# Gated recurrence and squared-ReLU network on one core: weights fetched ahead, a shorter decode, and VectorE's order written by hand

## The chip, the cores and the metric

The kernel runs on one core of one Trainium2 chip. The time is device microseconds of one execution; the median of several is compared. The engines are TensorE (PE; its weight loads are PEld in the profile), VectorE (DVE), ScalarE (ACT), GpSimd (POOL) and SyncE (SP), which here only issues transfers. Each engine takes its instructions in its own order and waits on semaphores for the others.

## The reference

Two parts follow one another. The first is a gated recurrence over 4 sequences of 768 steps with 8 heads of width 48; the second a feed-forward network on the 3072 tokens.

```python
mag = np.sqrt(a_re * a_re + a_im * a_im)
scale = np.minimum(mag, 0.999) / (mag + 1e-06)
a_re_n, a_im_n = (a_re * scale, a_im * scale)
for t in range(S):
    new_re = ar * S_re - ai * S_im          # ar, ai: the gates of step t, per head and row
    new_im = ar * S_im + ai * S_re
    S_re, S_im = (new_re + k[t] (x) v[t], new_im)
    y[:, :, t] = q[t] @ S_re
...
x = y as (3072 tokens, 384)
h = np.maximum(x @ w_in, 0.0)               # w_in: 384 x 2048
out = (h * h) @ w_out                       # w_out: 2048 x 384
```

`w_in` and `w_out` come as 64-bit floats; all else is 32-bit.

## The kernel before

`quotient_path` does the work; `general_path` is a second version, entered at the end only when some gate lies outside the range in which quotients of running products are exact enough (`good` counts the partitions where all is in range).

**Groups.** A chunk is 128 steps of one sequence, with its 8 heads side by side. A group is two chunks, of two sequences; there are 12 groups. `make_operands(gi)` (L515) prepares a group on VectorE with a little help of ScalarE: the inverse magnitude of the gates, two scans of the clamped scale (`u`, `v`), running complex products of the gates in blocks of 8 steps (the steps with tile `pr`), then over blocks (four `cmul` levels), then across (`carry` and one large `cmul`), and last the operands `qk`. What of `qk` belongs to rows that share a partition with other heads goes through SP transfers to the tiles `last` and `prod`. `chunk(gi, b)` (L592) then has TensorE make the scores `a_ps` (L613), VectorE mask them to `a`, TensorE add them into `y` (L621) beside the contribution of the running state (L606), and ScalarE copy `y` to `x` (L626). For the next chunk TensorE transposes the keys (`tp`, L634), sums them with the values (`add`, L645), and VectorE updates `state`. `fill_gaps(i)` (L669) moves rows of `x` into the gaps by six SP transfers; after it `first_product(i)` (L676: TensorE into `h_ps`, ScalarE Relu and Square) and `second_product(i)` (L689: TensorE into `o_ps`, ScalarE copy, SP store) can run.

**Weights.** After group 0's attention `load_w1` and `load_w2` fetch the weights as words and `decode` (L449) turns each 64-bit float into a 32-bit one with seven VectorE instructions: 12 tiles of 512 columns for `w_in`, 16 of 384 for `w_out`, through two buffers of words.

**Order.** The program is written in one order, and a planner places the instructions of every engine by that order as a priority and by expected times; each engine then runs its list in order. PSUM has two banks each for `a_ps`, `h_ps` and the tiles `tp` and `add`, one each for `y` and `o_ps`. `raw`, which holds a group's inputs, has two buffers, so that `load(gi + 2)` may go when group gi's operands are done.

Of the kernel before, what the change touches and what calls it, by code (L numbers as in the profile page):

```python
# [33 lines left out]
A_RE, A_IM, Q, K, V = range(5)  # L34

# [310 lines left out]
def quotient_path(ctx, tc, feat, vtok, w_in, w_out, w1, w2, out, n_seq, good):  # L346
# [14 lines left out]
    NB = C // L  # L361
    assert C == P and DM == HH * NP * D == NG * P and PAD * NG == D and n_seq % GC == 0
# [5 lines left out]
    ops = ctx.enter_context(tc.tile_pool(name="ops", bufs=2))  # L368
# [8 lines left out]
    def rows(hh):  # L377
        return slice(hh * ROWS, hh * ROWS + D)

    def pads(hh):  # L380
        return slice(hh * ROWS + D, (hh + 1) * ROWS)
# [3 lines left out]
              for bp in range(n_seq // GC) for c in range(NCH)]  # L385

# [6 lines left out]
    def load(gi):  # L393
        for part in (slice(A_RE, Q), slice(Q, V)):
            for b, n in enumerate(groups[gi]):
                for hh in range(HH):
                    nc.sync.dma_start(out=raw[gi % 2][rows(hh), part, b],
                                      in_=feat[n, hh, :, part, 0:NG])
                    rest = feat[n, hh].rearrange("(g r) x p t -> g r x p t", g=NG)
                    for g in range(NG):  # L400
                        nc.sync.dma_start(out=raw[gi % 2][pads(hh), part, b, g],  # L401
                                          in_=rest[g, :, part, NG])
# [4 lines left out]
    load(0)  # L407
# [17 lines left out]
    last = [const.tile([P, 4, GC, C], F32, name=f"last{i}") for i in range(2)]  # L425
    prod = [const.tile([P, 2, GC, NP], F32, name=f"prod{i}") for i in range(2)]

# [8 lines left out]
    ends = const.tile([P, 2, NGR, SEG], F32, name="ends")  # L436


    def w1_views(w):
        cut = NG * HH * D  # L440
        main = w[0:cut].rearrange("(g hh d) f -> hh d g f", g=NG, hh=HH)
        rest = w[cut:DM].rearrange("(hh g r) f -> hh r g f", hh=HH, g=NG)
        return [(rows(hh), main[hh]) for hh in range(HH)] + [
            (pads(hh), rest[hh]) for hh in range(HH)]

    def w2_view(w):
        return w.rearrange("(fb p) m -> p fb m", p=P)

    def decode(dst, words, width):  # L449


        low, high = words[:, 0:width, 0], words[:, 0:width, 1]
        mant = nrm.tile([P, E], I32, tag="low", name="mant")[:, 0:width]
        nc.vector.tensor_scalar(out=mant, in0=high, scalar1=0xFFFFF, scalar2=0x100000,
                                op0=ALU.bitwise_and, op1=ALU.bitwise_or)
        value = mant.bitcast(F32)
        nc.vector.scalar_tensor_tensor(out=value, in0=low.bitcast(U32), scalar=2.0 ** -32,  # L457
                                       in1=mant, op0=ALU.mult, op1=ALU.add)
        power = nrm.tile([P, E], I32, tag="high", name="power")[:, 0:width]
        nc.vector.tensor_scalar(out=power, in0=high, scalar1=20, scalar2=0x7FF,  # L460
                                op0=ALU.logical_shift_right, op1=ALU.bitwise_and)
        nc.vector.tensor_scalar(out=power, in0=power, scalar1=896, scalar2=896 + 255,
                                op0=ALU.max, op1=ALU.min)
# [33 lines left out]
    def tt(out, in0, in1, op):  # L497
        nc.vector.tensor_tensor(out=out, in0=in0, in1=in1, op=op)  # L498
# [286 lines left out]
```

## Time and profile before

| | |
|---|---|
| median of 3 runs | 856.02 us (853.28 to 858.97) |
| the profiled execution | 858.16 us, span 856.2 us |
| busy in the span: PE, DVE, ACT, POOL | 720.8, 528.4, 248.2, 33.3 us |
| mean granted TensorE clock | 0.919 |
| from HBM, to HBM | 36.18 MB, 4.72 MB |

The span is what the profile shows between its first and last event; about 2 us lie around it. In a row of a timeline stand start and length in us, engine, line of the kernel, operation, output and inputs, and the count of merged instructions; the bracket behind it tells how long the engine was idle before and what released it. In a group's row stand busy time and the mean of one instruction in ns, then the idle time ahead of such instructions. Most VectorE instructions have line 498, that of the helper `tt`, and are told apart by their tiles.

### The profile page before, as it was taken

How to read it: one execution, taken by the hardware profiler on the slowest of the kernel's cores; microseconds unless marked ns; L12 is line 12 of the kernel's file. 1: busy time of each engine (PE TensorE's matmuls, PEld its weight loads, DVE VectorE, ACT ScalarE, POOL GpSimd, SP SyncE). 2: the span in 40 equal slices, each digit the busy share in tenths (PEclk: the TensorE clock that was granted, in tenths of full speed). 3: DMA queues.
4: the chain of work that ended last, by engine and by line, in shares of the span. 5: the costliest groups of instructions: out<-in, count | busy, mean ns of one | idle time of the engine just before them, and what ended most of it. 6: DMA issues, size and time to landing. Idle time of an engine off the chain costs nothing.

```text
span 856.2 us, 11195 instructions
## 1 busy us (share of the span) xinstructions
PE 720.8 (84%) x4154; PEld 536.5 (63%) x4154; DVE 528.4 (62%) x1131; ACT 248.2 (29%) x446; POOL 33.3 (4%) x44
## 2 busy tenths in 40 slices
PE   0035575579399999889999999999999999999997
PEld 0034353136378687577686776867868778678683
DVE  4993899989989989778977494793854002010000
ACT  3021121013225144325052351532613314114140
POOL 3100000020000100000100010010000000000000
PEclk9975677569689999989999999999999999999999
DMA  4323554413131132213222231221101100000000
GB/s 109 76 65 75 125 146 129 129 49 82 44 88 33 30 97 57 64 36 84 60 73 67 62 74 39 40 73 33 33 9 37 17 19 5 10 10 5 19 0 24
DMA packets 76095, 47.66 MB, mean 56 GB/s; under 512 B 40576, under 2 KB 72448, under 8 KB 76032
## 3 DMA queue, kind: packets, MB, share of 16 engines
q1 hardware_dynamic: 76032, 46.86, 21.8%
q8 instruction: 35, 0.57, 0.3%
q14 instruction: 28, 0.23, 0.1%
HBM read 36.18 MB, written 4.72 MB: 48 GB/s over the span
## 4 chain that ended last, share of the span: by engine, by line
PE 56%; DVE 28%; SPq 7%; DMA 4%; ACT 3%; issue 2%; DVEq 0%; ACTq 0%
PE o_ps L693 21%; PE h_ps L682 20%; PE a_ps L613 5%; DVE raw L498 5%; PE y L621 4%; DVE pr L498 4%; PE y L606 3%; SPq L401 2%; DVE sq L541 2%; DMA words<-in_moe_w_in_dram 2%; PE add L645 2%; DVE power L466 2%; DVE qk L498 2%; DVE mant L457 1%; DVE w L468 1%
## 5 line engine op out<-in xcount | busy, mean ns | idle before, releaser
L682 PE MATMUL h_ps<-x,w 128*128 128x256 f32 x1152 | 273.8, 396 | 27.5 <-DVE w L468 26.1
L693 PE MATMUL o_ps<-w,h 128*128 128x384 f32 x768 | 269.7, 506 | 21.3 <-DVE w L468 20.3
L682 PEld LDWEIGHTS h_ps<-x,w 128*128 128x128 f32 x1152 | 223.7, 197 | 68.7 <-issue 16.9
L693 PEld LDWEIGHTS o_ps<-w,h 128*128 128x128 f32 x768 | 147.1, 196 | 131.1 <-DVE w L468 28.1
L498 DVE TENSOR_TENSOR a<-a_ps,mask 128x512 f32<-128x512 f32 x48 | 31.4, 685 | 143.0 <-PE a_ps L613 142.8
L685 ACT ACTIVATE h<-h_ps 128x512 f32<-128x512 f32 x96 | 57.0, 594 | 146.5 <-PE h_ps L682 146.4
L613 PE MATMUL a_ps<-qk 48*128 48x128 f32 x576 | 54.3, 300 | 44.3 <-DVE qk L498 44.3
L498 DVE TENSOR_TENSOR pr<-raw 128x384 f32<-128x384 f32 x84 | 72.0, 857 | 21.1 <-DMA raw<-in_feat_dram 19.3
L613 PEld LDWEIGHTS a_ps<-qk 48*128 48x128 f32 x576 | 46.0, 203 | 51.8 <-DVE qk L498 44.3
L686 ACT ACTIVATE h<-h 128x512 f32<-128x512 f32 x96 | 60.4, 630 | 2.8
L696 ACT COPY o<-o_ps 128x384 f32<-128x384 f32 x24 | 11.5, 479 | 160.8 <-PE o_ps L693 160.6
L621 PE MATMUL y<-a,vt 128*64 128x128 f32 x384 | 40.4, 304 | 18.6 <-DVE a L498 18.4
L544 POOL COPY ends<-sq 128x6 f32<-128x6 f32 x24 | 25.8, 1074 | 587.8 <-DVE sq L541 553.5
L621 PEld LDWEIGHTS y<-a,vt 128*64 128x64 f32 x384 | 28.1, 150 | 29.1 <-DVE a L498 24.0
L606 PE MATMUL y<-qk,state_mm 128*128 128x128 f32 x240 | 34.9, 293 | 13.3 <-DVE qk L498 13.2
L498 DVE TENSOR_TENSOR raw<-pr 128x96 f32<-128x96 f32 x168 | 44.8, 331 | 1.7
L751 DVE CAST count<-number 1x1 int32<-1x1 f32 x1 | 0.1, 147 | 72.5 <-PE number L750 72.5
L498 DVE TENSOR_TENSOR qk<-raw 128x1536 f32<-128x1536 f32 x24 | 41.2, 1753 | 5.3 <-PE a_ps L613 5.2
L606 PEld LDWEIGHTS y<-qk,state_mm 128*128 128x128 f32 x240 | 32.5, 204 | 18.9 <-issue 13.4
L626 ACT COPY x<-y 128x512 f32<-128x512 f32 x24 | 14.1, 587 | 60.1 <-PE y L621 60.0
L645 PE MATMUL add<-vt,kt 128*64 128x48 f32 x640 | 28.4, 230 | 1.6 <-ACT kt L636 1.6
L645 PEld LDWEIGHTS add<-vt,kt 128*64 128x64 f32 x640 | 26.3, 144 | 5.0 <-ACT kt L636 2.4
(300 smaller groups left out, 598.7 us busy)
## 6 DMA issues: line engine op xcount, KB each, us to landing
raw<-in_feat_dram SPq DMA_DIRECT2D x96, 144.0 KB, 2.6
words<-in_moe_w_out_dram SPq DMA_DIRECT2D x16, 384.0 KB, 3.0
raw<-in_feat_dram SPq DMA_DIRECT2D x288, 16.0 KB, 2.0
vt<-in_vtok_dram SPq DMA_DIRECT2D x24, 192.0 KB, 3.2
last<-qk SPq DMA_DIRECT2D x72, 64.0 KB, 2.4
words<-in_moe_w_in_dram SPq DMA_DIRECT2D x24, 192.0 KB, 3.4
out_dram<-o SPq DMA_DIRECT2D x24, 192.0 KB, 1.9
words<-in_moe_w_in_dram SPq DMA_DIRECT2D x24, 64.0 KB, 3.3
```

Of the source, the lines that this page charges most:

```text
L401: nc.sync.dma_start(out=raw[gi % 2][pads(hh), part, b, g], in_=rest[g, :, part, NG])
L466: nc.vector.scalar_tensor_tensor(out=power, in0=high, scalar=-2 ** 31, in1=power, op0=ALU.bitwise_and, op1=ALU.bitwise_or)
L498: nc.vector.tensor_tensor(out=out, in0=in0, in1=in1, op=op)
L544: nc.gpsimd.tensor_copy(out=ends[:, i, gi], in_=x.rearrange("p (s t) -> p s t", t=C)[:, :, C - 1])
L606: nc.tensor.matmul(y[:, p_], lhsT=s[:, c, p_].rearrange("p hh e -> p (hh e)"), rhs=operand(c, p_, slice(0, P)), start=(p_ == 0 and c == RE ...
L613: nc.tensor.matmul(ps[hh][:, p_], lhsT=operand(2 + c, p_, rows(hh)), rhs=operand(c, p_, rows(hh)), start=(c == RE), stop=(c == IM))
L621: nc.tensor.matmul(y[hh * ROWS:(hh + 1) * ROWS, p_], lhsT=v[:, HH * p_ + hh], rhs=am[hh][:, p_], start=(first and p_ == 0), stop=(p_ == NP ...
L645: nc.tensor.matmul(add[rr, c, p_], lhsT=kt[c][:, p_, rr], rhs=v[:, HH * p_ + hh, 0:D], start=True, stop=True)
L682: nc.tensor.matmul(ps[:, j], lhsT=w1[:, g, (2 * f + j) * P:(2 * f + j + 1) * P], rhs=x_of[i][:, g], start=(g == 0), stop=(g == NG - 1))
L685: nc.scalar.activation(out=h, in_=ps, func=AF.Relu)
L686: nc.scalar.activation(out=h, in_=h, func=AF.Square)
L693: nc.tensor.matmul(ps, lhsT=h_of[i][f // 2][:, f % 2, b * C:(b + 1) * C], rhs=w2[:, f], start=(f == 0), stop=(f == NFB - 1))
```

## The change

- **Loads.** `load` moves all four inputs of a chunk in one transfer per half (and one per gap piece), where there were two. For group 0 the gates come first, their gap pieces issued by ScalarE.
- **Words.** Weights come in 16 blocks of 768 columns (256 columns of `w_in` in its three row groups, or two row groups of `w_out`) through three buffers; the first three are fetched at the start, and each decoded block fetches the one three further on.
- **Decode.** Five VectorE instructions instead of seven. It is right only for weights of moderate size, so ScalarE watches the range: a Square and an Abs_reciprocal_sqrt per block, each with a sum, go into `sizes`, which enters `good`. `general_path` now decodes the weights again by the old seven instructions (`decode_weights`), inside the branch.
- **Operands.** The seven steps in blocks stand between the parts of the magnitude chain instead of behind it. The gate product at a chunk's end is a 129th column of `qk` and travels with `last`, so the transfers of `prod` go; ScalarE copies it to `prod`. The copies of `ends` move from GpSimd to ScalarE.
- **Order.** `chunk` pauses at two points. For groups 0 and 1 VectorE's order is as written: blocks of `w_in` are decoded among the pieces of group 0's attention, blocks of `w_out` among those of group 1's, where each decoded block at once goes into second product 0, for both chunks, in two accumulators (`po`'s bank and one of the two of `ph`). From group 2 on the planner orders VectorE as before.

```diff
-    def load(gi):
-        for part in (slice(A_RE, Q), slice(Q, V)):
-            for b, n in enumerate(groups[gi]):
...
+    def load(gi):
+        load_parts(gi, slice(A_RE, V), nc.sync)
+        load_values(gi)
+
+    load_parts(0, slice(A_RE, Q), nc.scalar)
+    load_parts(0, slice(Q, V), nc.sync)
+    load_values(0)
     load(1)
...
+        nc.vector.tensor_scalar(out=head, in0=high, scalar1=3, scalar2=0x3FFFFFF8,
+                                op0=ALU.logical_shift_left, op1=ALU.bitwise_and)
+        nc.vector.scalar_tensor_tensor(out=head, in0=high, scalar=-2 ** 30, in1=head,
                                        op0=ALU.bitwise_and, op1=ALU.bitwise_or)
+        nc.vector.tensor_scalar(out=rest, in0=head, scalar1=-2 ** 23, scalar2=None,
+                                op0=ALU.bitwise_and)
+        rest = rest.bitcast(F32)
+        nc.vector.scalar_tensor_tensor(out=rest, in0=low.bitcast(U32), scalar=2.0 ** -52, in1=rest,
+                                       op0=ALU.mult, op1=ALU.mult)
+        tt(dst, head.bitcast(F32), rest, ALU.add)
+        size = nrm.tile([P, E], F32, tag="z", name="size")
+        nc.scalar.activation(out=size, in_=high.bitcast(F32), func=AF.Square,
+                             accum_out=sizes[:, 0, j:j + 1])
+        nc.scalar.activation(out=size, in_=size, func=AF.Abs_reciprocal_sqrt, bias=tiny,
+                             accum_out=sizes[:, 1, j:j + 1])
...
+        words = words_of[j] = dec.tile([P, E, 2], I32, name="words", bufs=3)
...
+    def weights(j):
+        if j in words_of:
+            k = j - NBLK
+            decode(w1[:, :, j * BLK:(j + 1) * BLK] if k < 0 else
+                   w2[:, 2 * k:2 * k + 2].rearrange("p k m -> p (k m)"), words_of[j], j)
+        if j + 3 < 2 * NBLK:
+            fetch(j + 3)
+
+    for j in range(3):
+        fetch(j)
...
         for hh in range(HH):
             for g in range(NG):
                 at = slice(hh * ROWS + g * PAD, hh * ROWS + (g + 1) * PAD)
-                nc.sync.dma_start(out=last[gi % 2][at], in_=qk[pads(hh), :, :, g])
-                nc.sync.dma_start(out=pd[at, :, :, NG:NP], in_=pd[pads(hh), :, :, g:g + 1])
+                nc.sync.dma_start(out=last[gi % 2][at, :, :, 0:C + 1],
+                                  in_=qk[pads(hh), :, :, g, 0:C + 1])
+        nc.scalar.copy(out=pd[:, :, :, 0:NG], in_=qk[:, 0:2, :, :, C])
+        nc.scalar.copy(out=pd[:, :, :, NG], in_=last[gi % 2][:, 0:2, :, C])
...
+    def attention_among(gi, others):
+
+        make_operands(gi)
+        first, second = [chunk(gi, b) for b in range(GC)]
+        for step, n in ((first, 3), (first, 0), (second, 2), (second, 0), (first, 1), (second, 0)):
+            next(step, None)
+            for _ in range(n):
+                next(others)
+        load(gi + 2)
+        fill_gaps(gi)
...
+    def second_weights():
+        for b, pool, tag in ((0, po, "o"), (1, ph, "h")):
+            banks[b] = pool.tile([P, DM], F32, tag=tag, name="o_ps")
+        for j in every:
+            weights(NBLK + j)
+            for b in range(GC):
+                second_product(0, b, banks[b], [j])
+            yield
+
+    with tc.manual_schedule(engines={mybir.EngineType.DVE}):
+        others = first_weights()
+        attention_among(0, others)
+        first_product(0, every[:6])
+        for j in every[6:]:
+            next(others)
+            first_product(0, [j])
+        others = second_weights()
+        attention_among(1, others)
+        for j in every[6:]:
+            next(others)
+            first_product(1, every[4 * (j - 6):4 * (j - 6) + 4])
+        for b in range(GC):
+            store(0, b, banks[b])
+    for gi in range(2, NGR + 1):
+        if gi < NGR:
+            attention(gi)
+        if gi > 2:
+            first_product(gi - 1, every)
+        for b in range(GC):
             ps = po.tile([P, DM], F32, tag="o", name="o_ps")
...
+            second_product(gi - 1, b, ps, every)
+            store(gi - 1, b, ps)
```

More of the change, by code (lines that the diff above doesn't have):

```diff
@@ L436, in quotient_path @@
     ends = const.tile([P, 2, NGR, SEG], F32, name="ends")
[L439 to L463, printed above, removed]
-        nc.vector.tensor_scalar(out=power, in0=power, scalar1=896, scalar2=2 ** 23,
-                                op0=ALU.subtract, op1=ALU.mult)
-        nc.vector.scalar_tensor_tensor(out=power, in0=high, scalar=-2 ** 31, in1=power,
-                                       op0=ALU.bitwise_and, op1=ALU.bitwise_or)
-        nc.vector.scalar_tensor_tensor(out=dst, in0=value, scalar=2.0 ** -20,
-                                       in1=power.bitcast(F32), op0=ALU.mult, op1=ALU.mult)
@@ L699, in quotient_path @@
[L699 to L714 removed]
+            h_of[i, f] = h
```

269 lines of the change are left out of this document (171 added, 98 removed).

## The prediction

> **What bounds the kernel now.** I read the busy line and the 40 slices of the page first, then TensorE's windows, then the order of time around the places where it starts and stops.
>
> ```profile
> PE 720.8 (84%) x4154; PEld 536.5 (63%) x4154; DVE 528.4 (62%) x1131; ACT 248.2 (29%) x446; POOL 33.3 (4%) x44
> PE   0035575579399999889999999999999999999997
> DVE  4993899989989989778977494793854002010000
> ...
> 245.00:851.00 606.00, 597.88 (x3511) 454.02 (x3508) 323.21 (x683) 200.91 (x363) 16.02 (x16) 0.99 0.17 41
> ...
> 360.00:380.00 20.00, 14.76 (x168) 12.49 (x165) 17.25 (x48) 4.45 (x12) 0.51 (x2) 0.83 0.19 33
> ```
>
> The first two rows of digits are busy tenths in slices of 21.4 us. The shares mislead: VectorE (DVE) is full in the first half, TensorE (PE) in the second. In a window row the first pair after the length is PE's busy time, the third is DVE's, and the number behind the five pairs is the granted clock. From 245 us to the end PE is busy 597.88 of 606 us at clock 0.99. No edit here takes matmuls away, so that block stays; what can change is when it begins. Of the 8 us lost in it, 5.2 lie in one stretch (360 to 380).
>
> ```profile
> 87.90 0.43 DVE L454 TENSOR_SCALAR mant<-words 128x512 int32<-128x512 int32 x1 [10.94 <-DMA words<-in_moe_w_in_dram]
> 91.55 0.43 DVE L454 TENSOR_SCALAR mant<-words 128x512 int32<-128x512 int32 x1
> 91.61 2.04 PE L682 MATMUL h_ps<-x,w 128*128 128x256 f32 x4 [13.94 <-DVE w L468]
> 133.12 0.36 DVE L454 TENSOR_SCALAR mant<-words 128x384 int32<-128x384 int32 x1
> 136.10 0.36 DVE L454 TENSOR_SCALAR mant<-words 128x384 int32<-128x384 int32 x1
> 180.26 0.56 DVE L468 SCALAR_TENSOR_TENSOR w<-mant,power 128x384 f32<-128x384 f32 x1
> 218.94 3.78 SPq L674 DMA_DIRECT2D x<-x  x6
> 231.42 2.90 PE L606 MATMUL y<-qk,state_mm 128*128 128x128 f32 x12 [13.21 <-DVE qk L498]
> 245.47 5.65 PE L682 MATMUL h_ps<-x,w 128*128 128x256 f32 x16
> ```
>
> What delays the block: VectorE decodes all 28 weight tiles in one run, 87.90 to 180.82, that is 92.9 us (3.65 us for a tile of 512, 2.98 for one of 384, from start to start). In that time PE has only group 0 to feed on. Group 1's x gets its gap rows at 218.94 to 224; then PE, which takes its instructions in order, waits 13.21 us for group 2's qk, and group 1's first product runs densely only from 245.47.
>
> **The change, part by part.** *Decode.* Five instructions on 768 columns, 16 blocks, instead of seven on 512 or 384, 28 tiles.
>
> ```profile
> L522 DVE SCALAR_TENSOR_TENSOR sq<-sq 128x768 f32<-128x768 f32 x12 | 11.5, 956 | 17.0 <-ACT sq L520 17.0
> L498 DVE TENSOR_TENSOR z<-z,sq 128x768 f32<-128x768 f32 x12 | 11.4, 951 | 0.0
> L528 DVE TENSOR_SCALAR sq<-sq 128x768 f32<-128x768 f32 x12 | 6.6, 553 | 0.0
> L526 ACT ACTIVATE sq<-z 128x768 f32<-128x768 f32 x12 | 10.1, 843 | 0.2
> L526 ACT ACTIVATION_READ_ACCUMULATOR sq<-z 128x1 f32 x12 | 2.3, 192 | 0.0
> ```
>
> Two TENSOR_SCALAR at 0.55 and three two-input ones at 0.95 make 3.95 us; each needs the one before, which cost about 0.03 us apiece in the old decode, so 4.1 us a block and 65.6 us in all, 27 less than 92.9. The new integer forms are not in the trace: had the two TENSOR_SCALAR the two-input rate, it would be 13 us more; with the overlap that independent neighbours show (0.87 from start to start), 9 less. I take 4.1, since the old integer forms ran like the float ones. The watch on ScalarE is two passes and two accumulator reads, 2.1 us a block, 33 us in all; it lies beside VectorE's 4.1 us, on an engine busy 29%. Without that cover it would hold the words' buffer and with it the fetch three blocks on. Its first pass also waits for the words to land; behind it on ScalarE then stand the kt, x and Relu copies, for whom TensorE waits. With blocks fetched three ahead I put that at 0, at worst the 3 us of the late fetch below, once more.
>
> *Order.* I lay VectorE's new order out in time.
>
> ```profile
> 9.70 0.85 DVE L498 TENSOR_TENSOR pr<-raw 128x384 f32<-128x384 f32 x1 [8.50 <-DMA raw<-in_feat_dram]
> 18.14 1.35 SPq L401 DMA_DIRECT2D raw<-in_feat_dram  x3
> 40.82 3.42 DVE L498 TENSOR_TENSOR qk<-raw 128x1536 f32<-128x1536 f32 x2
> 395.33 0.86 DVE L498 TENSOR_TENSOR pr<-raw 128x384 f32<-128x384 f32 x1 [1.71 <-DMA raw<-in_feat_dram]
> 398.34 0.96 DVE L522 SCALAR_TENSOR_TENSOR sq<-sq 128x768 f32<-128x768 f32 x1 [2.15 <-ACT sq L520]
> 424.38 0.86 DVE L498 TENSOR_TENSOR raw<-p__3384,w__3385 128x672 f32<-128x672 f32 x1
> 535.90 0.56 DVE L498 TENSOR_TENSOR state<-add,state 128x384 f32<-128x384 f32 x1 [2.29 <-PE add L645]
> 537.56 0.63 DVE L498 TENSOR_TENSOR state<-p__3479,w__3480 128x192 f32<-128x192 f32 x2
> 539.66 1.29 DVE L498 TENSOR_TENSOR a<-a_ps,mask 128x512 f32<-128x512 f32 x2 [1.47 <-PE a_ps L613]
> 596.52 1.29 DVE L498 TENSOR_TENSOR a<-a_ps,mask 128x512 f32<-128x512 f32 x2 [1.47 <-PE a_ps L613]
> 78.39 3.77 SPq L674 DMA_DIRECT2D x<-x  x6
> ```
>
> One group's operands, taken where they run alone: 395.33 to 426.0 (the last instruction is one of a pair), less a wait of 2.15, plus 3.4 for qk: 31.9 us. A chunk's two masks take 1.3, its state 2.3 (1.7 for a sequence's first chunk).
>
> The first gates landed at 9.70 behind 16 issues on SP. Now SP issues four and ScalarE the twelve gap pieces at 0.45 each (1.35 for three): 5.4 us, then about 2.0 to land, so 8.2. No DMA issued by ScalarE is in the trace; the bounds are no gain and 1.5 us, and I take 1.5. It needs nothing more of SP: the merged load has 18 issues for 34, and SP is not late after this.
>
> Operands of group 0: 8.2 + 31.9, plus 2.4 for ScalarE's two table loads and its square, which the writes of step 1 wait for: 42.5 (before, 44.2). Three blocks: 54.8. Masks: 56.1. Two blocks: 64.3, and 3 for a late fetch: block 3's fetch may go only when block 0 is decoded (46.6) and its watch has read the words, and SP may have put 6 issues of `last` and 16 of group 2's load ahead of it, some 11 us from 42.5; four issues (0.42 each) and a landing of 3.4 follow. If they stand behind it, the stall is 0; if group 2's load also holds the DMA engines, 6. So 67.3; masks 68.6, state 70.3, block 74.4, state 76.1, two blocks 84.3. First product 0 needs y, its copy and the gaps (3.8 issue, 1.8 landing), about 77; its 96 matmuls end near 103, free of VectorE. Operands of group 1: 116.2. Three blocks 128.5, masks 129.8, two blocks 138.0, masks 139.3, and 3 for TensorE's scores being late (0 where its clock is full, 8 where it is half, below): 142.3. A wait here holds everything behind it, since VectorE's order is now fixed: state, the last three blocks, and with them group 2's operands. From there x of group 1: y and copy 2.5, gaps 5.6: 150.4. VectorE goes on with state, block, state, two blocks (16.9) to 159.2 and has group 2's operands at 191.1.
>
> *The sum.* The dense block begins at 150.4 for 245.5: 95 us earlier. What lies in it beyond the old one, from the rows that follow (the first three are windows of PE alone, so its clock stands right behind the one pair; they serve the rivals too):
>
> ```profile
> 142.00:180.00 38.00, 20.58 (x26) 0.52 0.42 124
> ...
> 99.00:101.00 2.00, 2.00 (x5) 0.50 0.79 213
> 103.00:105.00 2.00, 1.91 (x9) 1.00 0.91 234
> ...
> 151.04 1.65 PE L693 MATMUL o_ps<-w,h 128*128 128x384 f32 x2 [1.34 <-DVE w L468]
> ...
> 507.56 10.48 PE L693 MATMUL o_ps<-w,h 128*128 128x384 f32 x32
> 808.94 20.02 PE L682 MATMUL h_ps<-x,w 128*128 128x256 f32 x92
> ```
>
> Group 2's score work that PE had done before 245, some 11 us between 231.4 and 245.5 on a mostly half clock (12 matmuls in 2.90), an estimated 6 at full; the last two blocks of second product 0, 8 matmuls at 0.33 (10.48 for 32): 2.6; one bank of h fewer until about 161, since the second accumulator sits in it: three pairs of blocks at 0.9, 2.7; x of group 2, which is due near 214 (191.1, six issues and landing of `last` 6.2, two chunks of masks and y some 9, copy and gaps 8) where PE is through at 212: 2. Together 13. (From 150.4 PE has that 2.6 and 2.7, the 96 and 64 matmuls of group 1, 20.9 + 21.0 by the last two rows, and group 2's attention, 15.0: two masks rows a group apart, 539.66 and 596.52, give 56.9 a group, less 41.9. That is until 212.) Against it half of the 8 us lost in the old block, 4, as VectorE no longer trails. The profiled execution took 858.2 (span 856.2 plus 2.0): 858.2 - 95 + 13 - 4 = 772. The median of the plain runs stands 2.1 below it: **770**.
>
> Costed at nothing: the `prod` transfers that go, since they share SP with `last` and nothing but the state waits for them; POOL's copies of ends, off the path; the end checks, beside the last products.
>
> **Rivals.** *The cold clock.* In the second group each block gives PE four matmuls per 4.1 us. The windows show what such a trickle did: 20.58 us busy of 38 at clock 0.52, with 1.65 us for two matmuls against 0.66 at full clock; a dense stretch needed four us (99 to 103) to reach 1.00. At half clock the 64 matmuls cost 53 us and both chunks up to twice their 15.0, 83 in a window of 34 (116 to 150; at full clock 36), so masks of chunk 1 wait some 8 us instead of 3 and products spill over. A backlog is dense and warms itself, which caps it: 10 to 20 us more, 785. The Trainium skill, "TensorE: Matmul & The Clock Gate" (The HAM clock gate), says that the clock is released after one sustained busy window of about 3.4 us and falls back after an idle one; the rows agree, and by that rule the trickle stays cold.
>
> *ScalarE stuck behind a store.* The copy of `prod` now stands on ScalarE and reads `last`, six issues (0.6 each) and 2.4 us of landing after qk. If it stands ahead of a group's Relu or o copies, PE fills its two banks and stops. SP is in order too:
>
> ```profile
> SPq L697 <- ACT o L696: 261.4, 23, 29.8
> last<-qk SPq DMA_DIRECT2D x72, 64.0 KB, 2.4
> ```
>
> SP's store waits for the o copy, up to 29.8 us. Where `last` is queued behind a store, ScalarE could lose a whole o product, 10.5 us, in each of groups 3 to 11: 95 us, 865, slower than before. It decides from 86/9 = 9.6 us a group. Against it: 29% busy, and the waiting copy is placed in order of expected time. A mild form, 3 us a group, gives 797.
>
> *The order isn't kept.* If group 1's masks still come after all blocks, only the decode's 27 and a few us at the start go: 828.
>
> *Nothing stalls.* Without the two stalls of 3, the bank and the wait for x: 759. The floor is near 752: x of group 0 at 77, behind it 12 x 41.9 and 11 x 15.0 of PE work, 668, and 7 to the end of the execution, as now (851 to 858).
>
> **Chances.** Forecast (764 to 780) 0.50; nothing stalls 0.18; cold clock 0.16; mild ScalarE wait 0.07; order not kept 0.04; stuck behind the store 0.05. Range 750 to 805: it leaves out the last two and the ends of others. Faster by over 1% (about what a measurement of this kernel can tell from no change) 0.93, within 1% 0.02, slower 0.05.
>
> **What would show it.** Decode groups of 0.55 and 0.95 us and no block over 4.3; first dense first product of group 1 near 150, its busy row to the end over 98%; `a` masks in the second group waiting under 4 us for scores; granted clock between 116 and 150 (0.5: the cold rival); ScalarE's waits on a DMA into `last`, and PE idle on ACT inside each group (the store rival). Wrong it would be above all if PE's order, which nobody writes by hand, puts work of a later group ahead of what is ready.

## The result: 823.7 us, and where the 54 missing us are

The changed kernel takes 823.67 us (median of 4 runs, 823.48 to 824.74) against 855.72 of the kernel before on the same chip: ratio 0.963, interval 0.959 to 0.966. It is 32 us faster and 54 us slower than predicted. The profiled execution (823.65 us, span 821.9) has this page:

```profile
PE 695.2 (85%) x4154; PEld 531.9 (65%) x4154; DVE 497.7 (61%) x1020; ACT 287.0 (35%) x558; POOL 7.7 (1%) x22
PE   0074319979897998998999989989999999999997
DVE  4979999799798899999949479179113021010000
```

A slice is 20.5 us now. TensorE has a hole in its fourth to sixth slice, 62 to 123 us, where the prediction had first product 0; after it the nines are broken by eights and sevens up to the 27th slice, where the old kernel had a solid row.

The first part went as laid out. The timeline of VectorE shows the decode, a block every 4.16 us (predicted 4.1):

```profile
43.41 0.55 DVE L537 TENSOR_SCALAR both<-words 128x768 int32<-128x768 int32 x1
44.00 0.96 DVE L539 SCALAR_TENSOR_TENSOR both<-words,both 128x768 int32<-128x768 int32 x1
44.99 0.56 DVE L541 TENSOR_SCALAR both<-both 128x768 int32<-128x768 int32 x1
45.59 0.96 DVE L544 SCALAR_TENSOR_TENSOR both<-words,both 128x768 f32<-128x768 uint32 x1
46.58 0.96 DVE L459 TENSOR_TENSOR w<-both 128x768 f32<-128x768 f32 x1
47.57 0.56 DVE L537 TENSOR_SCALAR both<-words 128x768 int32<-128x768 int32 x1
```

Then two things go wrong, which the timelines of SP, TensorE, ScalarE and VectorE show in this order:

```profile
77.05 0.47 SPq L471 DMA_DIRECT2D raw<-in_feat_dram  x1
...
89.82 1.33 SPq L481 DMA_DIRECT2D vt<-in_vtok_dram  x2
91.21 4.25 SPq L775 DMA_DIRECT2D x<-x  x6
```

```profile
95.59 7.36 PE L782 MATMUL h_ps<-x,w 128*128 128x256 f32 x24 [21.66 <-DMA x<-x]
120.95 18.70 PE L782 MATMUL h_ps<-x,w 128*128 128x256 f32 x72 [17.99 <-ACT h L785]
```

```profile
111.55 0.51 ACT L661 COPY carry<-raw 128x180 f32<-128x180 f32 x1 [8.86 <-DVE raw L459]
116.86 1.48 ACT L619 ACTIVATE sq<-raw 128x1536 f32<-128x1536 f32 x1 [4.80 <-DVE raw L459]
118.25 0.19 ACT L682 COPY prod<-qk 128x12 f32<-128x12 f32 x1
...
120.32 0.58 ACT L785 ACTIVATE h<-h_ps 128x512 f32<-128x512 f32 x1
```

SP issues the load of group 2 (77 to 91) ahead of the six gap transfers of x of group 0. So the first product starts at 95.6, fills its two PSUM banks with 24 matmuls, and stops: the Relu that would empty them is at 120.32 on ScalarE, behind the copy of `carry` for group 1 and the Square for group 2, which wait for VectorE's steps (8.86 and 4.80 us), and behind two us of the weight watch. The product ends at 139.5. TensorE takes its work in order too, so group 1's scores come after it:

```profile
143.45 1.29 DVE L459 TENSOR_TENSOR a<-a_ps,mask 128x512 f32<-128x512 f32 x2
...
157.88 0.17 DVE L868 TENSOR_SCALAR sizes<-sizes 128x16 f32<-128x16 f32 x1 [4.93 <-ACT size L548]
...
159.25 1.28 DVE L459 TENSOR_TENSOR a<-a_ps,mask 128x512 f32<-128x512 f32 x2
```

The masks of group 1 end at 145 and 160.5 instead of 130 and 142, and the dense products of group 1 begin at 174.7 instead of 150.4. (The wait at `sizes`, an end check that the planner laid ahead of the second masks, cost them about 1 us: their last scores were made at 158.4.) The other half of the miss lies behind that. The window from there to the last o copy, two of the waits in it, and their row in TensorE's list of waits (us in total, times, longest):

```profile
174.74:816.53 641.79, 613.85 (x3635) 467.76 (x3633) 349.61 (x738) 216.80 (x420) 0.00 (x0) 0.98 0.22 40
```

```profile
210.47 0.69 PE L721 MATMUL y<-a,vt 128*64 128x128 f32 x2 [3.96 <-DVE a L459]
258.87 0.69 PE L721 MATMUL y<-a,vt 128*64 128x128 f32 x2 [5.75 <-DVE a L459]
```

```profile
PE y L721 <- DVE a L459: 26.7, 13, 5.7
```

The block is 642 us where the sum had 614 (605 of the old block, plus 13, less 4). TensorE idles 28 us in it, mostly waiting for a mask (21.9 of the run's 26.7 us lie in the block). 24 us of later start and 27 of longer block are the error; the last 2 us are the step from the profiled execution to the median, which the sum took off and which is not there now. The experiments show that the two parts don't simply add.

### The profile page after: what moved, and what is told of

Same layout as the page of the kernel before. It is cut to its first block, busy times and chain, and to the rows that moved or that the text cites. A ratio compares the mean times of both kernels' runs of the same rounds, so it can differ in the third digit from the quotient of the medians.

```text
span 821.9 us, 10849 instructions
## 1 busy us (share of the span) xinstructions
PE 695.2 (85%) x4154; PEld 531.9 (65%) x4154; DVE 497.7 (61%) x1020; ACT 287.0 (35%) x558; POOL 7.7 (1%) x22
## 4 chain that ended last, share of the span: by engine, by line
PE 59%; DVE 31%; DMA 3%; issue 3%; ACT 3%; SPq 1%; ACTq 0%; DVEq 0%
PE h_ps L782 25%; PE o_ps L793 22%; DVE raw L459 6%; DVE pr L459 5%; DVE sq L644 4%; PE a_ps L712 4%; PE y L721 3%; PE add L745 2%; DMA raw<-in_feat_dram 2%; PE y L705 2%; DVE a L459 2%; DVE qk L459 2%; DVE sq L459 1%; DVE both L544 1%; DVE state L459 1%
## 5 line engine op out<-in xcount | busy, mean ns | idle before, releaser
L782 PE MATMUL h_ps<-x,w 128*128 128x256 f32 x1152 | 262.5, 386 | 40.6 <-DMA x<-x 21.7
L782 PEld LDWEIGHTS h_ps<-x,w 128*128 128x128 f32 x1152 | 219.6, 193 | 75.6 <-issue 24.1
L793 PE MATMUL o_ps<-w,h 128*128 128x384 f32 x768 | 255.7, 491 | 4.3 <-DVE w L459 3.2
L793 PEld LDWEIGHTS o_ps<-w,h 128*128 128x128 f32 x768 | 145.2, 191 | 101.5 <-DVE w L459 3.3
L785 ACT ACTIVATE h<-h_ps 128x512 f32<-128x512 f32 x96 | 57.1, 594 | 91.6 <-PE h_ps L782 91.2
L712 PE MATMUL a_ps<-qk 48*128 48x128 f32 x576 | 51.1, 301 | 43.5 <-DVE qk L459 43.5
L712 PEld LDWEIGHTS a_ps<-qk 48*128 48x128 f32 x576 | 43.5, 203 | 49.8 <-DVE qk L459 43.5
L721 PE MATMUL y<-a,vt 128*64 128x128 f32 x384 | 41.6, 318 | 26.8 <-DVE a L459 26.7
L644 DVE TENSOR_TENSOR_SCAN sq<-sq,both 128x128 f32<-128x128 f32 x144 | 46.9, 400 | 1.1 <-ACT both L635 0.9
L745 PE MATMUL add<-vt,kt 128*64 128x48 f32 x640 | 34.4, 247 | 5.2 <-ACT kt L736 5.0
L745 PEld LDWEIGHTS add<-vt,kt 128*64 128x64 f32 x640 | 31.3, 160 | 9.5 <-ACT kt L736 8.2
L765 ACT COPY state_mm<-state 48x384 f32<-48x384 f32 x40 | 20.4, 509 | 41.8 <-DVE state L459 41.6
```

The lines of the kernel that those rows point to most:

```text
L644: nc.vector.tensor_tensor_scan(out=x[:, at], data0=x[:, at], data1=y[:, at], initial=1.0, op0=ALU.mult, op1=ALU.mult)
L712: nc.tensor.matmul(ps[hh][:, p_], lhsT=operand(2 + c, p_, rows(hh)), rhs=operand(c, p_, rows(hh)), start=(c == RE), stop=(c == IM))
L721: nc.tensor.matmul(y[hh * ROWS:(hh + 1) * ROWS, p_], lhsT=v[:, HH * p_ + hh], rhs=am[hh][:, p_], start=(first and p_ == 0), stop=(p_ == NP ...
L745: nc.tensor.matmul(add[rr, c, p_], lhsT=kt[c][:, p_, rr], rhs=v[:, HH * p_ + hh, 0:D], start=True, stop=True)
L765: nc.scalar.copy(out=state_mm[b][rows(hh), :, :, hh, 0:D], in_=new[rows(hh)])
L782: nc.tensor.matmul(ps[:, j], lhsT=w1[:, g, (2 * f + j) * P:(2 * f + j + 1) * P], rhs=x_of[i][:, g], start=(g == 0), stop=(g == NG - 1))
```

## The experiments

All kernels are the changed one with the edit named. The block is the time from the first dense product of group 1 to the last o copy, in the profiled execution, with the busy time of TensorE and VectorE in it (in before and planner_order a few matmuls of group 1's first product run scattered ahead of it); the ratio is to the kernel before on the same chip, with its 95% interval.

| run | first product 0 from | block from | block | PE busy | DVE busy | median | ratio |
|---|---|---|---|---|---|---|---|
| before | 91.6 | 245.5 | 605 | 597 | 323 | 855.7 | |
| changed | 95.6 | 174.7 | 642 | 614 | 350 | 823.7 | 0.963 (0.959 to 0.966) |
| gaps_first | 82.2 | 158.8 | 654 | 624 | 356 | 820.3 | 0.960 (0.958 to 0.963) |
| relu_by_hand | 95.2 | 170.4 | 648 | 610 | 344 | 824.6 | 0.965 (0.962 to 0.969) |
| old_steps | 97.7 | 180.8 | 647 | 619 | 353 | 834.3 | 0.975 (0.971 to 0.979) |
| masks_by_hand | 94.8 | 174.1 | 639 | 618 | 365 | 821.2 | 0.962 (0.959 to 0.965) |
| store_on_act | 95.4 | 175.2 | 637 | 614 | 348 | 818.0 | 0.955 (0.950 to 0.959) |
| load_in_halves | 98.8 | 174.3 | 639 | 616 | 350 | 820.1 | 0.957 (0.953 to 0.961) |
| gaps_and_store | 82.2 | 159.3 | 640 | 616 | 355 | 813.5 | 0.952 (0.948 to 0.956) |
| gaps_store_masks | 81.9 | 155.4 | 645 | 619 | 370 | 809.8 | 0.947 (0.942 to 0.951) |
| gaps_store_masks_relu | 82.0 | 156.9 | 645 | 622 | 369 | 808.6 | 0.946 (0.943 to 0.950) |
| gaps_store_masks_pool | 82.0 | 156.6 | 655 | 627 | 369 | 815.8 | 0.951 (0.948 to 0.955) |
| braided | 82.0 | 155.4 | 651 | 624 | 368 | 817.2 | 0.957 (0.951 to 0.964) |
| planner_order | 88.7 | 216.9 | 629 | 604 | 319 | 853.8 | 0.998 (0.996 to 0.999) |
| planner_gaps_store | 88.7 | 208.4 | 637 | 612 | 340 | 852.0 | 0.995 (0.992 to 0.997) |
| longer_decode | 102.7 | 190.3 | 647 | 617 | 352 | 845.6 | 0.987 (0.983 to 0.990) |
| light_operands | 94.7 | 172.8 | 629 | 611 | 271 | 808.4 | 0.943 (0.939 to 0.947) |
| very_light | 94.2 | 173.9 | 605 | 602 | 159 | 786.2 | 0.918 (0.915 to 0.921) |
| very_light_gaps_store | 82.0 | 153.4 | 606 | 603 | 165 | 766.6 | 0.895 (0.892 to 0.898) |
| ballast | 95.5 | 179.0 | 645 | 617 | 304 | 833.5 | 0.975 (0.973 to 0.978) |

The profiled execution of gaps_and_store, 805.5 us, was the fastest of its five (805.5 to 816.9), so its row shows the kernel at its best.

### The late start: SP's order and ScalarE's

**gaps_first**

```diff
-        load(gi + 2)
         fill_gaps(gi)
+        load(gi + 2)
```

> The changed kernel, with the gap transfers of x issued before the load two groups on (one line moved in attention_among). Theory A (SP's order is what made x of group 0 late, and the planner put the Relus of first product 0 behind ScalarE's copies for group 1 only because it, too, saw x late): the gaps of group 0 go out near 80 instead of 91, the 96 matmuls run without the 18 us hole and end before 112 instead of 139.5, the first dense product of group 1 starts near 160 instead of 174.7, and the time is 808 to 812 (823.7 less some 14). Rival B (ScalarE's copies hold the Relu whatever SP does): the hole stays over 12 us, 818 to 824. Rival C (what an earlier start brings is given back, since VectorE then trails further behind in the groups after it): the start moves to 160, but the block from there to the end grows from 642 to over 652, and the time is 818 to 823.

**relu_by_hand**

```diff
+        with tc.manual_schedule(engines={mybir.EngineType.Activation}):
+            make_operands(gi, between)   # one first_product(0, [j]) at a time between its parts
```

> The changed kernel, SP's order as it was, but ScalarE's order by hand in group 1's operands: a Relu of first product 0 after each of the steps, instead of all of them behind ends, carry and prod. x of group 0 is as late as before (95). Theory A' (ScalarE's order alone costs the 18 us hole): the hole goes, the 96 matmuls end near 123 instead of 139.5, the masks of group 1's first chunk run near 134 instead of 143.5, the dense product starts 8 to 10 us earlier, 813 to 817. Rival (the hole goes, but VectorE's decode sets the second group anyway, or the start is given back later): 821 to 826.

The rows of TensorE, first of gaps_first, then of relu_by_hand:

```profile
82.15 7.58 PE L782 MATMUL h_ps<-x,w 128*128 128x256 f32 x24 [8.66 <-DMA x<-x]
92.87 4.54 PE L782 MATMUL h_ps<-x,w 128*128 128x256 f32 x12 [3.14 <-ACT h L785]
```

```profile
95.22 23.61 PE L790 MATMUL h_ps<-x,w 128*128 128x256 f32 x96 [20.91 <-DMA x<-x]
119.35 1.60 PE L713 MATMUL y<-qk,state_mm 128*128 128x128 f32 x12 [0.53 <-DVE qk L459]
```

Either edit closes the hole (gaps_first but for three waits of at most 3.14 us): theories A and A' are right about its cause. With x early the planner itself puts the Relus among the copies, so SP's order was the root and ScalarE's the consequence. But the time hardly moves. gaps_first starts the block 16 us earlier and lengthens it by 12 (rival C: 820.3); relu_by_hand starts 4 us earlier and gains nothing (its rival). What an earlier start brings is given back in the block.

Even gaps_first starts 8 us behind the prediction's 150.4. VectorE's order by hand fixes only the order of the instructions written there among each other; the planner lays group 2's operand steps between them. In the changed kernel's rows the decode blocks of group 1 stand 5.0 and 6.3 us apart, not 4.1, with such steps in them:

```profile
120.19 0.55 DVE L537 TENSOR_SCALAR both<-words 128x768 int32<-128x768 int32 x1
120.66 0.33 DVE L459 TENSOR_TENSOR raw<-pr 128x96 f32<-128x96 f32 x1
...
125.19 0.56 DVE L537 TENSOR_SCALAR both<-words 128x768 int32<-128x768 int32 x1
...
131.47 0.56 DVE L537 TENSOR_SCALAR both<-words 128x768 int32<-128x768 int32 x1
```

In gaps_first they do the same. Where most of group 2's steps are left out the block begins 6 us earlier (very_light_gaps_store, 153.4, against gaps_and_store, 159.3).

### The long block: order

**old_steps**: `steps_in_blocks(range(1, L))` in one run behind the products with `u` and `v`, `ends` and `prod` copied by GpSimd.

> The changed kernel, with the steps of the running products in one run after the normalisation and the copies of ends and prod on GpSimd, as in the kernel before; the hand order, the decode and the loads stay. It tells why the block from the first dense product to the end takes 642 us instead of 606. Theory D (the new order of the operand steps, and the copies on ScalarE, delay the masks): the block falls to 612 to 625 and the time to 795 to 808. Rival E (the masks are late because VectorE is full for its first 230 us in either form, and the planner's places for the masks don't fit): the block stays at 636 to 646, the time 816 to 830.

The block did not shrink (647), and its start was 6 us later: theory D falls, and block and time lie just above rival E's numbers. The new order and the copies on ScalarE together are worth 10.6 us as they stand.

**masks_by_hand**

```diff
+    with tc.manual_schedule(engines={mybir.EngineType.DVE}):
         for gi in range(2, NGR + 1):
             if gi < NGR:
                 attention(gi)
```

> The changed kernel, with VectorE's order by hand in groups 2 to 11 as well: the operands of a group whole, then its masks and states, then the next group's operands. Theory E (TensorE's waits of 1.5 to 5.8 us for a mask come from the places among the operand steps that the planner gave the masks): these waits nearly go, the block falls from 642 to 612 to 625, the time to 798 to 808. Rival F (VectorE now waits for TensorE's scores with everything behind it, and a group's operands come late in their turn): VectorE has 37 us of work in a group of 57, so one wait of over 20 us in a group would show, and the time is 825 to 850.

```profile
PE y L705 <- DVE qk L459: 13.5, 8, 3.3
PE y L721 <- DVE a L459: 5.4, 3, 3.2
```

That is from its list of waits. The waits for masks went from 26.7 us to 5.4, as theory E wanted, and waits for the operands came in their place, 13.5 us. VectorE waits 12.8 us a group for scores before it may go on, and groups follow at 58.6 us, as two rows of its masks show:

```profile
545.86 1.29 DVE L459 TENSOR_TENSOR a<-a_ps,mask 128x512 f32<-128x512 f32 x2 [12.77 <-PE a_ps L712]
...
604.48 1.29 DVE L459 TENSOR_TENSOR a<-a_ps,mask 128x512 f32<-128x512 f32 x2 [12.78 <-PE a_ps L712]
```

Neither theory's number: 821.2.

**store_on_act** and **load_in_halves**

```diff
-        nc.sync.dma_start(out=out[n * C:(n + 1) * C], in_=o)
+        nc.scalar.dma_start(out=out[n * C:(n + 1) * C], in_=o)
```

```diff
-        load_parts(gi, slice(A_RE, V), nc.sync)
+        load_parts(gi, slice(A_RE, Q), nc.sync)
+        load_parts(gi, slice(Q, V), nc.sync)
```

> The changed kernel, with the store of o issued by ScalarE, right behind its copy, instead of by SP. In the changed kernel VectorE waited 11.07, 16.13 and 22.87 us for raw in groups 5 to 7 (423, 478 and 540 us), while SP stood at a store that waits for the o copy, with the last gap pieces of the merged load behind it; in the kernel before the same first step waited 1.7 us. Theory G (the merged load has no early half: its last pieces stand behind the store, operands come 16 to 23 us late, and TensorE runs out of products to lay beside the scores): these waits fall under 5 us, the two groups that took 62 us from o to o (473.4 to 597.6) take 57 again, and the time is 808 to 814. Rival H (VectorE's late start there lies in its slack; the 62 us come from the masks' places): the waits go and the time stays at 820 to 825.

> The changed kernel, with the load of groups 1 to 11 in two halves again, the gates first and then q and k (each still with merged rows); the stores stay on SP. One part of the change undone. Theory G: the gates are whole before SP reaches the store, VectorE's waits for raw fall under 5 us as in the kernel before, and the time is 808 to 815, though SP issues 16 more transfers a group (some 7 us of its time). Rival H: 820 to 826.

VectorE's start of a group's operands near 478, in the changed kernel and then in store_on_act:

```profile
477.89 0.87 DVE L459 TENSOR_TENSOR pr<-raw 128x384 f32<-128x384 f32 x1 [16.12 <-DMA raw<-in_feat_dram]
```

```profile
463.00 0.87 DVE L459 TENSOR_TENSOR pr<-raw 128x384 f32<-128x384 f32 x1 [6.10 <-DMA raw<-in_feat_dram]
473.90 0.51 DVE L459 TENSOR_TENSOR raw<-pr 128x96 f32<-128x96 f32 x2 [10.03 <-ACT sq L619]
```

The wait changed hands. Without the store in front of the load, raw came 15 us sooner, and the first write then waited 10 us for ScalarE's Square, which stood behind an o copy that waited for TensorE. In halves, waits of 14 and 17 us for raw stayed too. So theory G was not put to the test it asked for: the edits brought 5.7 and 3.6 us, and in store_on_act the two groups that took 62 us from o to o still took 61.

Why a late start hurts an engine with time to spare is seen beside the kernel before, in the same stretch (before first, then changed):

```profile
540.86 3.42 DVE L498 TENSOR_TENSOR qk<-raw 128x1536 f32<-128x1536 f32 x2
...
549.67 0.96 DVE L522 SCALAR_TENSOR_TENSOR sq<-sq 128x768 f32<-128x768 f32 x1 [3.12 <-ACT sq L520]
...
589.19 1.29 DVE L498 TENSOR_TENSOR a<-a_ps,mask 128x512 f32<-128x512 f32 x2 [11.04 <-PE a_ps L613]
```

```profile
539.70 0.87 DVE L459 TENSOR_TENSOR pr<-raw 128x384 f32<-128x384 f32 x1 [22.87 <-DMA raw<-in_feat_dram]
...
550.81 2.30 DVE L644 TENSOR_TENSOR_SCAN sq<-sq,both 128x128 f32<-128x128 f32 x7
553.03 1.26 DVE L459 TENSOR_TENSOR a<-a_ps,mask 128x512 f32<-128x512 f32 x2
...
553.74 0.69 PE L721 MATMUL y<-a,vt 128*64 128x128 f32 x2 [2.28 <-DVE a L459]
```

Before, a group's steps, but for the first multiplication and `qk`, began after the masks (539.66 in the prediction's rows) and were through before the next, for which VectorE waited 11 us. Now they begin 13 us ahead of the masks, which stand among them, and TensorE waits for VectorE.

### Together

**gaps_and_store**, **gaps_store_masks** and **gaps_store_masks_relu** join the edits above.

> The changed kernel with both: the gap transfers of x issued before the load (820.3 by itself) and the store issued by ScalarE. Theory G and the lead: the 11 us that the gaps first brought at group 1 are no longer eaten later, 797 to 806. Rival C (VectorE's masks in the middle of operand steps eat the lead in groups 2 to 4 whatever the load does): 808 to 812, that is what the store alone brings.

> Those two and VectorE's order by hand in all groups (821.2 by itself). Theory: with the lead kept in groups 2 to 4 (no mask among operand steps) and the load early, the block runs at 57 us a group throughout, 788 to 800. Rival F (by hand VectorE waits 12.8 us a group for scores, and a group's operands then end after the products that should cover them, as in the 58.6 us from group to group that the hand order showed): 800 to 812.

> Gaps first, store on ScalarE, masks by hand in all groups (809.8), and the Relus of first product 0 by hand among group 1's operands too. With the gaps first the planner puts them early already (two waits of 3 us left in the first product). If those few us count: 804 to 808. If VectorE's time decides: 808 to 812.

The edits add up roughly: 3.4 and 5.7 alone, 10.2 together, 13.9 with the masks, 15.0 with the Relus (the last step is within the spread). All three missed their hopeful number and came out at their rivals' (813.5 just above). The last is the fastest full version found: 808.6 us, ratio 0.946 against 0.963 of the change.

**braided** lays the first half of the next group's operands between a group's masks (`for part in (others, first, others, first, others, second, others, second)`), and issues the gaps first in all groups, not only in 0 and 1; **gaps_store_masks_pool** moves the copies of `ends` and `prod` to GpSimd.

> Gaps first, store on ScalarE, and VectorE's order by hand in all groups, but with the first half of the next group's operands laid between a group's masks, so that VectorE has work while TensorE makes the scores (with the masks by hand and nothing between, groups followed each other at 58.6 us, with VectorE waiting 12.8 us for scores in each). Theory: the period falls to TensorE's own 56.6 us, no wait for qk, 795 to 805 (809.8 without the braid). Rival: a mask now stands behind up to 8 us of operand steps as in the planner's order, TensorE idles on masks again, 809 to 818.

> Gaps first, store on ScalarE, masks by hand (809.8), and the copies of ends and prod moved from ScalarE to GpSimd. In that run ScalarE stood 45 us at the copy of prod that waits for last, in six groups. If that wait holds the Relu and o copies for TensorE (the prediction's rival of ScalarE stuck, in its mild form): 800 to 806. If ScalarE has the time: 807 to 812.

Both are slower than gaps_store_masks, by 7 and 6 us. The braid's rival holds as a time; its groups still followed at 59 us. Taking `prod` off ScalarE brought no gain, so its 45 us there look like time it had; a few us could hide behind the copies, which are dear on GpSimd (below).

### Which part brought the 32 us

**planner_order**: `attention(0)`, all 16 `weights(j)`, then the groups in a plain loop, no order by hand. **planner_gaps_store**: the same with the two edits of SP's order, the gaps first in all groups.

> The changed kernel without VectorE's order by hand: attention of group 0, all 16 decode blocks, then the groups one after the other, every engine in the planner's order; decode, loads and operand steps as changed. It tells which part of the change brought the 32 us. Theory I (the shorter decode and start bring most of it, the hand order little, since what it moves forward is given back in the groups after it): 822 to 832, at most 8 us behind the changed kernel; the prediction's rival gave 828. Theory J (the order by hand brings most of it): 838 to 850.

> The planner's order, with the gaps of x issued before the load and the store issued by ScalarE. Both together took 10 us from the hand order. Theory G (they are faults of SP's order whatever orders VectorE): 8 to 12 us under the run without them, 812 to 822. Rival K (they matter only where TensorE's dense part starts early): under 4 us.

Without the order by hand the change is worth 2 to 3 us. Theory J was nearest and still too low. In planner_order the decode ends at 152 instead of 181 and x of group 1 is 26.5 us earlier; the dense products begin at 217 instead of 245, and TensorE waits 36.1 us for masks in the run (15.9 of them at once, in group 0, ahead of the block):

```profile
PE y L721 <- DVE a L459: 36.1, 14, 15.9
```

```profile
216.87:845.50 628.63, 604.13 (x3502) 459.53 (x3498) 319.43 (x689) 207.47 (x400) 0.00 (x0) 0.98 0.21 38
```

The block takes 629 where the old one took 605, and eats most of it. Mending SP's order there gives 1.7 us, within the spread (rival K).

**longer_decode**

```diff
-        tt(dst, head.bitcast(F32), rest, ALU.add)
+        for _ in range(2):
+            tt(dst, head.bitcast(F32), rest, ALU.add)
+        nc.vector.tensor_scalar(out=rest, in0=rest, scalar1=1.0, scalar2=None, op0=ALU.mult)
```

> The changed kernel with two instructions added to each decode block (the last sum once more, and one multiplication by 1 in place): about 1.5 us a block, 24 us in all, nearly the 27 us by which the change shortened the decode. It tells what the shorter decode is worth under the hand order. If each microsecond of VectorE ahead of group 1's x counts (13 of the 16 blocks lie there): 19 to 24 us slower, 842 to 848. Theory O (time ahead of the block is mostly given back in it, as in the planner's order, where x of group 1 was 26.5 us earlier than in the kernel before and the end 5.5): 826 to 834.

21.9 us slower: theory O falls here. Under the hand order VectorE's time ahead of the block counts nearly in full when it is added, though the 11 us by which gaps_first was ahead (last decode at 169.8 instead of 180.7) brought only 3.4 at the end. Why the two directions differ was not settled.

### The long block: VectorE's time

**light_operands**: `for j in js if gi < 2 else ()` in `steps_in_blocks`. **very_light** leaves out more, **very_light_gaps_store** has SP's two edits as well, and **ballast** puts three multiplications per step back whose results are not used.

> The changed kernel with the seven steps of the running products inside blocks left out in groups 2 to 11 (some 9 us of VectorE's 37 a group). Theory L (TensorE idles 28 us in the block because VectorE, behind after the two groups, has masks queued behind its operand steps): idle time on masks falls by half, the block from 642 to 620 to 630, the time to 802 to 813. Rival M (it is the order on SP and ScalarE, not VectorE's load): block 636 to 644, time 817 to 825.

> The changed kernel with the steps, the totals, the scans and the carrying-in left out in groups 2 to 11; normalisation, qk, masks and states stay, so VectorE has some 13 us a group instead of 37. Theory L (the block is 27 us longer than the prediction's sum because VectorE's operand steps stand ahead of masks; with 9 us less a group it fell from 641.8 to 629.1): the block falls to 616 to 622, the prediction's 605 + 13 and less, TensorE idles under 12 us in it, and the time is 794 to 803. Rival N (the rest of the idle time comes from the order on ScalarE, SP and TensorE itself): the block stays at 625 to 630, 805 to 811.

> The same, with the gaps first and the store on ScalarE. If the late x of groups 0 and 1 and VectorE's steps among the masks are the whole of what the prediction missed (770), this run comes near it: dense products of group 1 from 155 to 159, a block of 616 to 622, 776 to 786. If the earlier start is given back even with a light VectorE, 790 to 800.

> The very light kernel (786.2) with 21 multiplications of 0.85 us put back on VectorE in groups 2 to 11 (some 18 us a group), whose results nobody reads: they only need the group's raw. If VectorE's time as such makes the block 37 us longer (masks and qk come later whenever VectorE has 31 us or more in a group), the block goes from 605 back to 630 to 642 and the time to 811 to 824. If it is the length of the operands' own chain (steps, waits between VectorE and ScalarE, carry) that comes back late, and not the time on the engine, the block stays under 615 and the time under 796.

The blocks of the four, in this order:

```profile
172.78:801.85 629.07, 610.70 (x3635) 464.73 (x3633) 270.88 (x549) 217.42 (x420) 0.00 (x0) 0.99 0.22 41
```

```profile
173.88:778.65 604.77, 602.19 (x3635) 457.66 (x3633) 159.06 (x244) 213.47 (x416) 0.00 (x0) 1.00 0.23 43
```

```profile
153.44:759.10 605.66, 603.20 (x3634) 457.50 (x3634) 165.49 (x253) 215.93 (x422) 0.00 (x0) 1.00 0.25 45
```

```profile
179.03:823.54 644.51, 616.74 (x3635) 469.43 (x3633) 304.37 (x432) 213.97 (x416) 0.00 (x0) 0.97 0.22 40
```

With the same start (174) and 190 us less on VectorE, the block is 605 us, at clock 1.00 and with under 3 us of idle TensorE: better than theory L hoped, in time too (786.2). Of the 37 us, 25 are idle time of TensorE (28 us against 3) and 12 are a longer busy time for the same matmuls (614 against 602): in the changed kernel the granted clock was 0.72 from 200 to 220 us and 0.91 to 0.94 from there to 280, in very_light 1.00 all along. With a light VectorE the early start is no longer given back: SP's two edits then bring 19.6 us instead of 10.2, and the time is 766.6, under what the text ahead of the run gave and beside the 770 of the prediction. Time put back that nobody depends on, 145 us of it in the block, brings the long block back. So VectorE's work costs the 37 us, and the operands' own chain is not needed for it. Ballast's multiplications wait for `raw` as well, 105 us in five waits where the changed kernel has 59, so the run doesn't separate how long that work is from how late it starts.

It is not the amount alone. The kernel before has 323 us of VectorE in its block, and TensorE idles 8 us; ballast has 304, and it idles 28. What VectorE holds when the scores arrive seems to matter; no run isolates it. An order of the full work by hand that keeps both the masks and the operands on time was not found here (two were tried, 645 and 651 us), and whether there is one stays open.

## Why the prediction was wrong

- **Start, decode, group 0: right.** Gates landed at 8.9 (predicted 8.2), decode 4.16 us a block (4.1), the eight blocks of `w_in` done at 87.3 (84.3), operands of group 1 at 120.3 (116.2), of group 2 at 195.3 (191.1). These points of VectorE's timeline held within about 4 us, though not the order between the last two: group 2's steps ran among group 1's blocks, not behind them.
- **"x of group 0 ready about 77": wrong by 18.** The step counted six issues and their landing, and left out what SP has in its list ahead of them: group 2's load and late words. "SP is not late after this" had been worked out for the words, not for x. gaps_first has the product at 82.2, so 13 of the 18 us are group 2's load.
- **"Its 96 matmuls end near 103, free of VectorE": the step that failed** in the start, by 36 us, half of it the late x and half the hole. The matmuls need no VectorE; the Relu that frees their banks stood behind `carry` and Square on ScalarE, which do. Two us more were passes of the watch, put at nothing. The Trainium skill, "PSUM — Partial Sum Buffer" (Engine vs sequencer instructions), says that ScalarE's queue is strictly first in, first out; the wait of 17.99 us for a Relu whose input was ready agrees. The prediction named such a rival, ScalarE stuck, but at `prod` and a store in the later groups, where it was not seen; a store did hold SP there, but ahead of `raw` (5.7 us in store_on_act).
- **Masks of group 1 and the start of the block:** 145 and 160.5 instead of 130 and 142, 174.7 instead of 150.4. 16 of these 24 us go with the gaps first; in what is left are group 2's steps, which "VectorE's order is now fixed" had behind the last blocks. The cold clock was not the reason. The window of the second group shows 0.84, not 0.5, with TensorE busy 29 of 34 us, since the delayed product ran there in one piece. In gaps_first, where that product was through by 114, it shows 0.80 and 31 us (second row). So the trickle of that rival did not come about in either. (In the block a lower clock goes with the 12 us of longer busy time above.)

```profile
116.00:150.00 34.00, 29.05 (x141) 23.47 (x142) 33.38 (x67) 20.59 (x40) 0.00 (x0) 0.84 0.54 121
```

```profile
116.00:150.00 34.00, 30.96 (x220) 22.86 (x221) 32.77 (x59) 17.76 (x38) 0.00 (x0) 0.80 0.53 137
```

- **"+13, -4" for the block: the dearer step that failed**, 36 us instead of 9. Half of the old block's stalls was to go "as VectorE no longer trails"; the reverse happened. The sum moved TensorE's block forward whole and never laid VectorE's list beside it. In the first 226 us of the block VectorE (third pair) is busy 92% of the time, and it waits for scores ahead of only one mask; 17 of TensorE's 28 idle us lie there, and 9 more between 480 and 600, after VectorE's waits of 16 and 23 us for `raw`. The gaps first alone bring 3.4 us, VectorE's work left out alone 37, both (with the store) 57. The very light runs show that the rest of the sum can be reached: 605 us, and 766.6 in all. That the latter lies beside 770 is in part luck, for its block begins 3 us later and is 9 us shorter than in the sum.

```profile
174.00:260.00 86.00, 75.60 (x440) 57.85 (x438) 79.57 (x167) 30.97 (x63) 0.00 (x0) 0.90 0.34 59
260.00:400.00 140.00, 132.97 (x856) 104.10 (x855) 129.53 (x269) 59.06 (x113) 0.00 (x0) 0.99 0.34 62
```

- **"The order isn't kept: 828": wrong by 26.** It counted the decode's 27 us in full; in the planner's order 2 to 3 of them came out as time.

Right was the direction, and that the order by hand is what counts. The floor of 752 and the 759 of the rival in which nothing stalls were not reached even with a light VectorE: 766.6.

## What to carry to other kernels

When work is moved forward on one engine, lay out every engine's list, not that of the engine moved: here issues on SP and a copy on ScalarE, whose lists nobody had written, kept a product of TensorE that needs no VectorE back by 36 us. A dense block could not be slid forward as a whole: ask how far ahead the feeding engine will be when it starts, and test it by taking that engine's work out (very_light) and putting idle work back (ballast) before tuning orders. An edit that removes a wait should be read by the next wait on the same row: store_on_act turned 16 us on a transfer into 6 on the transfer and 10 on ScalarE.

## What the runs showed of the hardware

Small copies are dear on GpSimd: 0.78 to 1.59 us. These rows group the copies by line, in gaps_store_masks_pool; on ScalarE the same copies took 0.2 us in the changed kernel (118.25 above).

```profile
L647 POOL COPY ends<-sq 128x6 f32<-128x6 f32 x24 | 30.4, 1268 | 411.3 <-DVE sq L644 375.0 <-ACT h L785 36.3
L682 POOL COPY prod<-qk 128x12 f32<-128x12 f32 x12 | 19.1, 1589 | 139.4 <-DVE qk L459 139.4
L683 POOL COPY prod<-last 128x4 f32<-128x4 f32 x12 | 9.3, 778 | 94.3 <-DMA last<-qk 94.3
```

VectorE's integer forms on 128x768, not in the trace of before, ran at the rate of the float ones: 0.55 us with one tensor input, 0.96 with two (43.41 to 46.58 above).
